# The first four blocks of a gated linear attention plus feed-forward kernel: loads split by tensor, stage list rewritten, y copied by ScalarE alone, two products of zeros at the start

## Chip, cores, metric

One core of one Trainium2 chip. The metric is the device time of one execution in microseconds; the kernel before takes 678.32 us (median of 678.15, 678.32 and 679.73).

## The reference

A linear attention with per-channel decay, written as a recurrence, then a feed-forward network with squared ReLU. All of it is float32; the weights come as float64 and are converted on the chip.

```python
# q, k, v, alpha: (B=4, H=8, S=768, D=48)
for t in range(S):
    state = alpha[:, :, t, :, None] * state + einsum('bhd,bhe->bhde', k[:, :, t], v[:, :, t])
    y[:, :, t] = einsum('bhd,bhde->bhe', q[:, :, t], state)
x = y.transpose(0, 2, 1, 3).reshape(3072, 384)
h = maximum(x @ w_in, 0)          # w_in (384, 2048)
out = (h * h) @ w_out             # w_out (2048, 384)
```

## The kernel before

The sequence is cut into 24 blocks of 128 steps (one chunk of one batch, all heads). A block has four stages: `decays` (transpose alpha, logarithm, running sum by a scan, two exponentials), `turn` (transpose q and k, scale them), `scores` (q times k, mask; k turned back into `ks`), `values` (state update `kv`, output `y`, copies of y into `xT`). Four blocks make a group of 512 tokens; while the feed-forward products of group g run, the stages of group g+1 are placed between them. Blocks 0 to 3 have no such products beside them: they are the start-up that this case is about. During the first feed-forward group (blocks 4 to 7) the weights are converted piece by piece, half on VectorE and half on ScalarE.

```python
NIN = 3; NV = 4; GB = 4; NR = 4
...
s_t = kept("s", B, [128, NP, 128])
for t in s_t:
    nc.vector.memset(t, 0.0)
...
def convert_first(i):          # a weight piece: DVE, DVE, then ACT, ACT
    nc.vector.tensor_scalar(out=power, in0=hi, ...)
    nc.vector.tensor_scalar(out=upper, in0=hi, ...)
    nc.scalar.activation(out=power, in_=power, func=AF.Relu, scale=2.0**23, bias=rebias)
    nc.scalar.activation(out=w, in_=lo, func=AF.Copy, scale=2.0**-52, bias=1.0)
def convert_second(i):         # then DVE three times
    nc.vector.scalar_tensor_tensor(out=power, ...)
    nc.vector.scalar_tensor_tensor(out=w, ...)
    nc.vector.tensor_tensor(out=w, in0=w, in1=power.bitcast(FP32), op=ALU.mult)

for n in range(NIN):
    load(n)                    # alpha, q, k, v of a block, 192 KB each
def next_weights():            # load piece, convert_second(i - 1), convert_first(i)
    ...
ident = consts.tile([128, 128], FP32, name="ident")
make_identity(nc, ident)       # POOL; every transpose needs it
...
def values(n):
    ...
    for p in range(NP):        # NP = 4 head pairs, one PSUM tile y
        copy = nc.scalar.copy if p < NP // 2 else nc.vector.tensor_copy
        for r, f, end in ((64, 2*p*D + 32, 2*(p + 1)*D), (0, 2*p*D, (2*p + 1)*D)):
            while f < end:     # 12 copies in all
                ...
                copy(out=xT[g][to:to+m, kk, t*C:(t+1)*C], in_=y[r:r+m, p, :])
...
order = [(0, 0), (0, 1), (1, 0), (0, 2), (1, 1)]
for n in range(2, GB):
    order += [(n - 2, 3), (n, 0), (n - 1, 2), (n, 1)]
order += [(GB - 2, 3), (GB - 1, 2), (GB - 1, 3)]
for n, s in order:
    stages[s](n)
    ...                        # further loads of inputs and weights
    if (n, s) in ((GB - 2, 3), (GB - 1, 2), (GB - 1, 3)):
        next_weights()
```

Of the kernel before, what the change touches and what calls it, by code (L numbers as in the profile page):

```python
# [8 lines left out]
FP32 = mybir.dt.float32  # L9
# [6 lines left out]
GB = 4  # L16
# [7 lines left out]
def kernel(  # L24
# [22 lines left out]
    nc = tc.nc  # L47
    B, H, S, D = q.shape
    C = 128
    NCH = S // C  # L50
    NP = H // 2
# [14 lines left out]
    ps_att = ctx.enter_context(tc.tile_pool(name="ps_att", bufs=4, space=PSUM))  # L66
# [4 lines left out]
    def kept(name, n, shape):  # L71
        return [consts.tile(shape, FP32, name=f"{name}{i}") for i in range(n)]

    NIN = 3
# [5 lines left out]
    tiles["v"] = kept("v_in", NV, [128, H * D])  # L80
    s_t = kept("s", B, [128, NP, 128])
    for t in s_t:
        nc.vector.memset(t, 0.0)


    srcs = {"a": alpha, "q": q, "k": k, "v": v}
# [1 line left out]
    def load(n, xs="aqkv"):  # L88
        c, b = divmod(n, B)
        for x in xs:  # L90
            t = tiles[x][n % len(tiles[x])]
            nc.sync.dma_start(
                out=t.rearrange("a (h d) -> a h d", h=H) if x == "v" else t[:, :, 0:D],
                in_=srcs[x][b, :, c * C : (c + 1) * C, :].rearrange("h s d -> s h d"),
            )
# [6 lines left out]
    def load_weights(i):  # L102
        dst = (w_in + w_out)[i]
        dt = moe_w_in.dtype
        raw = dst if dt == FP32 else raw_pool.tile(list(dst.shape), dt, tag="raw", name="raw")
        raws[i] = raw
        if i < NW:
            src = moe_w_in[:, i * DF // NW : (i + 1) * DF // NW]
            nc.sync.dma_start(out=raw, in_=src.rearrange("(k r) f -> r k f", r=128))
        else:  # L110
            i -= NW
            src = moe_w_out[i * DF // NW : (i + 1) * DF // NW, :]
            nc.sync.dma_start(out=raw, in_=src.rearrange("(j r) m -> r j m", r=128))
# [35 lines left out]
        )  # L149
        nc.vector.tensor_tensor(out=w, in0=w, in1=power.bitcast(FP32), op=ALU.mult)  # L150

    for n in range(NIN):
        load(n)
    to_load = list(range(2 * NW))
    stage = [0]

    def next_weights():
        i = stage[0]
        stage[0] += 1
        if NR - 2 <= i and to_load:  # L160
            load_weights(to_load.pop(0))
        if moe_w_in.dtype != FP32:
            if 0 < i <= 2 * NW:
                convert_second(i - 1)
            if i < 2 * NW:
                convert_first(i)


    nc.scalar.preload_act_table_set("natural_log_exp_and_others")
    ident = consts.tile([128, 128], FP32, name="ident")  # L170
    make_identity(nc, ident)
# [4 lines left out]
    nc.vector.memset(again[:, :, 0:1], 0.0)  # L176
    rebias = consts.tile([128, 1], FP32, name="rebias")
    nc.vector.memset(rebias, -896.0 * 2.0**23)
    NAM = 2
    am_t = kept("am", NAM, [128, 2, NP, 128])  # L180
    for t in am_t:
        nc.vector.memset(t, 0.0)


    bs, invs, qkT, ks, xT = {}, {}, {}, {}, {}
# [34 lines left out]
    def scores(n):  # L220
# [10 lines left out]
        for e in range(2):  # L231
            nc.vector.copy_predicated(  # L232
                out=am_t[n % NAM][:, e],
                mask=causal.bitcast(U32).unsqueeze(1).to_broadcast([128, NP, C]),
# [9 lines left out]
    def values(n):  # L244
        c, batch = divmod(n, B)
        qT = qkT.pop(n)[0]
        b = bs.pop(n)
        v_in = tiles["v"][n % NV]
        am = am_t[n % NAM]
        st = s_t[batch]  # L250
        kv = None
        if c < NCH - 1:
            kv = ps_att.tile([128, NP, 2 * D], FP32, tag="att", name="kv")
            kt = ks.pop(n)
            for p in range(NP):
                nc.tensor.matmul(  # L256
                    out=kv[:, p, :], lhsT=kt[:, p, :],
                    rhs=v_in[:, 2 * p * D : 2 * (p + 1) * D], start=True, stop=True,
                )
            pieces = []  # L260
            for e in range(2):
                rows = slice(64 * e, 64 * e + D)
                new = kv[rows, :, e * D : (e + 1) * D]
                old = st[rows, :, 80 * e : 80 * e + D]
                if c:
                    sm = p2.tile([128, NP, D], FP32, tag="sm", name="sm")
                    nc.vector.tensor_tensor(out=sm[rows], in0=new, in1=old, op=ALU.add)  # L267
                    new = sm[rows]
                pieces.append((old, new, b[rows, :, C - 1 : C].to_broadcast([D, NP, D])))

        y = ps_att.tile([128, NP, C], FP32, tag="att", name="y")
        if c:
            for p in range(NP):
                nc.tensor.matmul(  # L274
                    out=y[:, p, :], lhsT=st[:, p, :], rhs=qT[:, p, :],
                    start=(p == 0), stop=False, skip_group_check=True,
                )
        for p in range(NP):
            for e in range(2):
                nc.tensor.matmul(  # L280
                    out=y[64 * e : 64 * e + D + G * e, p, :],
                    lhsT=v_in[:, (2 * p + e) * D - G * e : (2 * p + e + 1) * D],
                    rhs=am[:, e, p, :], start=(c == 0 and p == 0), stop=True,
                    skip_group_check=True,
                )
        g, t = divmod(n, GB)
        if t == 0:
            xT[g] = x_pool.tile([128, KM, GB * C], FP32, tag="xT", name="xT")

        for p in range(NP):  # L290
            copy = nc.scalar.copy if p < NP // 2 else nc.vector.tensor_copy
            for r, f, end in ((64, 2 * p * D + 32, 2 * (p + 1) * D), (0, 2 * p * D, (2 * p + 1) * D)):
                while f < end:
                    kk, to = divmod(f, 128)
                    m = min(end - f, *(RUN[i % 128] for i in (r, to)))
                    copy(out=xT[g][to : to + m, kk, t * C : (t + 1) * C], in_=y[r : r + m, p, :])  # L296
                    r, f = r + m, f + m
        if kv is not None:
            for old, new, last in pieces:
                nc.vector.tensor_tensor(out=old, in0=new, in1=last, op=ALU.mult)  # L300
# [39 lines left out]


    stages = [decays, turn, scores, values]
    order = [(0, 0), (0, 1), (1, 0), (0, 2), (1, 1)]
    for n in range(2, GB):
        order += [(n - 2, 3), (n, 0), (n - 1, 2), (n, 1)]
    order += [(GB - 2, 3), (GB - 1, 2), (GB - 1, 3)]
    for n, s in order:
        stages[s](n)
        if (n, s) == (0, 1):
            load(3)  # L350
            load_weights(to_load.pop(0))
        if (n, s) == (1, 1):
            load(4, "a")
            load_weights(to_load.pop(0))
            load(4, "qk")
            load_weights(to_load.pop(0))
        if (n, s) == (0, 3):
            load(4, "v")
            load_weights(to_load.pop(0))
        if (n, s) in ((GB - 2, 3), (GB - 1, 2), (GB - 1, 3)):  # L360
            next_weights()

    NS = GB * len(stages)
    for g in range(NBLK // GB):
# [7 lines left out]
        for slot in range(NS):  # L372
            i, s = divmod(slot, len(stages))
            n = (g + 1) * GB + i
# [39 lines left out]
```

## Time and profile before

| | before |
|---|---|
| time, median of 3 | 678.32 us |
| profiled span, mean granted clock | 677.3 us, 0.977 |
| PE busy | 649.0 us (96%) |
| DVE, ACT busy | 275.2 us (41%), 194.4 us (29%) |
| first feed-forward product starts | 50.91 us |
| PE alone on the chain that ended last from | 118.50 us |

The shares of the whole span say little here, because they mix a start-up in which PE waits with a long stretch in which it never does. The view by slices shows the two: each digit is a fortieth of the span (17 us), in tenths. In the profile PE is TensorE, PEld its weight loads, DVE VectorE, ACT ScalarE, POOL GpSimd; PEclk is the clock granted to TensorE, as a share of full speed. Of the tiles, `la` is the logarithm of alpha and its running sum, `b` and `inv` the two exponentials, `am` the masked scores; `h` is the first feed-forward product, `r` its maximum with 0, `hid` the square of `r`, and `o` the second product.

```profile
PE   6768987999999999999999999999999999999998
PEclk9668999899999999999999999999999999999999
```

The first seven digits of PE are all there is to win; the other thirty-three are full, and the clock is full there too but for a dip in the eighth slice. The prediction shows the tables, waits and timelines that resolve those seven digits. In timeline lines the columns are start, length, engine, source line, operation, output and inputs, shape, count, and in brackets the idle time before and what ended it.

### The profile page before, as it was taken

To read this page: it belongs to the slowest core of one execution; us is meant where nothing else is said; L and a number is where in the kernel's file an instruction comes from. 1 tells how busy PE (TensorE), PEld (TensorE's weight loads), DVE (VectorE), ACT (ScalarE), POOL (GpSimd) and SP (SyncE) were. 2 spreads that over 40 slices of the span, in tenths; PEclk is the share of its full clock that TensorE was granted. 3 is DMA by queue.
4 is the path that set the end of the run, shared out by engine and by line. 5 is a ranking of instruction groups with operands and counts; after the bars stand their busy time and mean duration, and the time that the engine had idled before them with its cause. 6 is when DMAs were issued, how large, how long until landed. Compare 5 with 4: busy or idle time off the path is not lost.

```text
span 677.3 us, 7062 instructions
## 1 busy us (share of the span) xinstructions
PE 649.0 (96%) x2800; PEld 383.3 (57%) x2800; DVE 275.2 (41%) x505; ACT 194.4 (29%) x405; POOL 2.4 (0%) x17
## 2 busy tenths in 40 slices
PE   6768987999999999999999999999999999999998
PEld 5554544666555566554666655566645566644554
DVE  6658776865443331444422235412244422122100
ACT  3344666432332220332211223302223312122100
POOL 1000000000000000000000000000000000000000
PEclk9668999899999999999999999999999999999999
DMA  9916373800900012630003280003090000000000
GB/s 159 260 48 140 96 184 108 162 11 13 164 11 0 3 34 46 99 54 1 0 13 71 51 101 0 1 13 58 13 151 1 1 12 13 12 13 0 0 24 23
DMA packets 108705, 36.64 MB, mean 54 GB/s; under 512 B 100480, under 2 KB 103552, under 8 KB 108672
## 3 DMA queue, kind: packets, MB, share of 16 engines
q1 hardware_dynamic: 108672, 36.18, 28.4%
q8 instruction: 22, 0.36, 0.2%
q14 instruction: 11, 0.09, 0.0%
HBM read 31.46 MB, written 4.72 MB: 53 GB/s over the span
## 4 chain that ended last, share of the span: by engine, by line
PE 85%; DVE 8%; ACT 4%; issue 1%; DMA 1%; SPq 0%; DVEq 0%; ACTq 0%
PE o L326 37%; PE h L310 31%; PE y L280 3%; PE sc L226 3%; PE kv L256 2%; PE y L274 2%; PE kT L191 2%; DVE xT L296 2%; PE kr L240 2%; PE qT L191 1%; ACT xT L296 1%; DVE power L143 1%; PE aT L191 1%; DVE w_in L147 1%; DVE w_in L150 1%
## 5 line engine op out<-in xcount | busy, mean ns | idle before, releaser
L326 PE MATMUL o<-w_out,hid 128*128 128x384 f32 x768 | 257.7, 490 | 2.9 <-ACT r L315 2.9
L310 PE MATMUL h<-xT,w_in 128*128 128x512 f32 x576 | 256.9, 598 | 0.8 <-ACT xT L296 0.8
L326 PEld LDWEIGHTS o<-w_out,hid 128*128 128x128 f32 x768 | 143.4, 191 | 97.4 <-issue 3.7
L310 PEld LDWEIGHTS h<-xT,w_in 128*128 128x128 f32 x576 | 106.8, 191 | 122.6 <-issue 119.4
L319 DVE TENSOR_TENSOR hid<-r 128x512 f32<-128x512 f32 x80 | 55.4, 692 | 126.6 <-ACT r L315 126.3
L315 ACT ACTIVATE r<-h 128x512 f32<-128x512 f32 x96 | 56.9, 593 | 141.0 <-PE h L310 140.9
L296 DVE COPY xT<-y 32x128 f32<-32x128 f32 (+1 forms) x144 | 41.4, 288 | 83.5 <-ACT xT L296 80.6
L296 ACT COPY xT<-y 32x128 f32<-32x128 f32 (+1 forms) x144 | 37.1, 258 | 97.8 <-PE y L280 95.4
L334 ACT ACTIVATE osb<-o 128x384 f32<-128x384 f32 x24 | 11.8, 490 | 136.9 <-PE o L326 134.2
L232 DVE COPY_PREDICATED am<-causal,sc 128x512 f32<-128x512 uint32 x48 | 32.1, 723 | 42.9 <-PE sc L226 42.8
L201 DVE TENSOR_TENSOR_SCAN la<-again,la 128x512 f32<-128x512 f32 x24 | 29.3, 1222 | 32.5 <-ACT la L199 32.4
L226 PEld LDWEIGHTS sc<-qT,kT 48*128 48x128 f32 x384 | 24.7, 193 | 21.7 <-issue 11.8
L226 PE MATMUL sc<-qT,kT 48*128 48x128 f32 x384 | 29.8, 292 | 7.3 <-DVE kT L217 4.6
L256 PEld LDWEIGHTS kv<-v_in,ks 128*128 128x128 f32 x160 | 23.0, 212 | 11.7 <-ACT ks L242 6.7
L217 DVE TENSOR_TENSOR qT<-qT,b 128x512 f32<-128x512 f32 x24 | 16.6, 691 | 31.5 <-PE qT L191 30.4
L280 PE MATMUL y<-am,v_in 128*48 128x128 f32 (+1 forms) x384 | 28.5, 294 | 0.0
L135 ACT ACTIVATE power<-power,rebias 128x768 uint32<-128x768 uint32 x16 | 15.0, 936 | 46.5 <-DVE power L128 46.5
L256 PE MATMUL kv<-v_in,ks 128*128 128x96 f32 x160 | 23.7, 297 | 4.2 <-ACT ks L242 4.2
L267 DVE TENSOR_TENSOR sm<-kv,s 48x192 f32<-48x192 f32 x32 | 11.3, 354 | 38.7 <-PE kv L256 38.3
L208 ACT ACTIVATE b<-la 128x512 f32<-128x512 f32 x24 | 15.1, 630 | 35.9 <-DVE la L201 35.9
L280 PEld LDWEIGHTS y<-am,v_in 128*48 128x48 f32 (+1 forms) x384 | 22.4, 138 | 3.0 <-issue 0.5
L274 PE MATMUL y<-qT,s 128*128 128x128 f32 x160 | 21.6, 278 | 0.0
(42 smaller groups left out, 297.6 us busy)
## 6 DMA issues: line engine op xcount, KB each, us to landing
raw<-in_moe_w_in_dram SPq DMA_DIRECT2D x8, 768.0 KB, 5.4
raw<-in_moe_w_out_dram SPq DMA_DIRECT2D x8, 768.0 KB, 4.3
a_in<-in_alpha_dram SPq DMA_DIRECT2D x24, 192.0 KB, 4.9
q_in<-in_q_dram SPq DMA_DIRECT2D x24, 192.0 KB, 5.0
k_in<-in_k_dram SPq DMA_DIRECT2D x24, 192.0 KB, 4.9
v_in<-in_v_dram SPq DMA_DIRECT2D x24, 192.0 KB, 4.7
out_dram<-osb SPq DMA_DIRECT2D x24, 192.0 KB, 1.9
```

Source lines behind the costliest of these rows:

```text
L191: nc.tensor.transpose(out=ps[:, p, :], in_=rows[:, 128 * p : 128 * (p + 1)], identity=ident)
L201: nc.vector.tensor_tensor_scan(out=la.rearrange("a p t -> a (p t)"), data0=again.rearrange("a p t -> a (p t)"), data1=la.rearrange("a p t ...
L226: nc.tensor.matmul(out=ps[e][:, p, :], lhsT=kT[rows, p, :], rhs=qT[rows, p, :], start=True, stop=True,)
L232: nc.vector.copy_predicated(out=am_t[n % NAM][:, e], mask=causal.bitcast(U32).unsqueeze(1).to_broadcast([128, NP, C]), data=ps[e],)
L256: nc.tensor.matmul(out=kv[:, p, :], lhsT=kt[:, p, :], rhs=v_in[:, 2 * p * D : 2 * (p + 1) * D], start=True, stop=True,)
L274: nc.tensor.matmul(out=y[:, p, :], lhsT=st[:, p, :], rhs=qT[:, p, :], start=(p == 0), stop=False, skip_group_check=True,)
L280: nc.tensor.matmul(out=y[64 * e : 64 * e + D + G * e, p, :], lhsT=v_in[:, (2 * p + e) * D - G * e : (2 * p + e + 1) * D], rhs=am[:, e, p, ...
L296: copy(out=xT[g][to : to + m, kk, t * C : (t + 1) * C], in_=y[r : r + m, p, :])
L310: nc.tensor.matmul(out=ps, lhsT=w[:, kk, c0 : c0 + 128], rhs=xT[g][:, kk, :], start=(kk == 0), stop=(kk == KM - 1),)
L315: nc.scalar.activation(out=r, in_=ps, func=AF.Relu)
L319: nc.vector.tensor_tensor(out=hid[j], in0=r, in1=r, op=ALU.mult)
L326: nc.tensor.matmul(out=acc[t][:, 0:DM], lhsT=hid[j][:, t * C : (t + 1) * C], rhs=w_out[i][:, j % per, :], start=(j == 0), stop=(j == NJ - 1),)
```

## The change

The intent is to bring the first data to PE sooner, to keep PE's clock up while it waits for them, and to take VectorE's y copies out of the chain of the first groups. Its core (the moved loads of inputs and weights further down the start-up list are cut, and so is the move of `am`'s memsets to the front of VectorE's queue, which makes the zeros ready for the two products):

```diff
 for t in s_t:
-    nc.vector.memset(t, 0.0)
+    nc.gpsimd.memset(t, 0.0)
...
-for n in range(NIN):
-    load(n)
+for n, xs in ((0, "aqk"), (1, "a"), (0, "v"), (1, "qk"), (2, "a"), (1, "v"), (2, "qk")):
+    load(n, xs)
...
+for _ in range(2):
+    nc.tensor.matmul(
+        out=ps_att.tile([128, NP, C], FP32, tag="att", name="warm"),
+        lhsT=am_t[0][:, 0, 0, :], rhs=am_t[0][:, 0], start=True, stop=True,
+    )
...
-    for p in range(NP):
-        copy = nc.scalar.copy if p < NP // 2 else nc.vector.tensor_copy
+    for p in (1, 3, 0, 2):
+        on_scalar = p < NP // 2 or g < 2 and n != GB - 1
+        copy = nc.scalar.copy if on_scalar else nc.vector.tensor_copy
...
-order = [(0, 0), (0, 1), (1, 0), (0, 2), (1, 1)]
+order = [(0, 0), (0, 1), (1, 0), (0, 2), (1, 1), (0, 3)]
 for n in range(2, GB):
-    order += [(n - 2, 3), (n, 0), (n - 1, 2), (n, 1)]
+    order += [(n, 0), (n - 1, 2), (n, 1), (n - 1, 3)]
-order += [(GB - 2, 3), (GB - 1, 2), (GB - 1, 3)]
+order += [(GB - 1, 2), (GB - 1, 3)]
```

`g < 2` reaches further than the title's "first four blocks": blocks 4 to 7, the ones placed beside the first feed-forward group, get their y copies on ScalarE too. Only block 3 (`n == GB - 1`) and the blocks from 8 on keep the split, now in alternating order.

More of the change, by code (lines that the diff above doesn't have):

```diff
@@ L166, in next_weights @@
                 convert_first(i)
+    NAM = 2
+    am_t = kept("am", NAM, [128, 2, NP, 128])
+    for t in am_t:
+        nc.vector.memset(t, 0.0)
     nc.scalar.preload_act_table_set("natural_log_exp_and_others")
@@ L178 @@
     nc.vector.memset(rebias, -896.0 * 2.0**23)
-    NAM = 2
-    am_t = kept("am", NAM, [128, 2, NP, 128])
-    for t in am_t:
-        nc.vector.memset(t, 0.0)
+    for _ in range(2):
[3 more added lines that the diff above has]
+        )
     bs, invs, qkT, ks, xT = {}, {}, {}, {}, {}
@@ L349 @@
         if (n, s) == (0, 1):
-            load(3)
+            load(3, "a")
+            load(2, "v")
+            load(3, "qk")
+            load_weights(to_load.pop(0))
+            load(3, "v")
             load_weights(to_load.pop(0))
@@ L355 @@
             load(4, "qk")
+        if (n, s) == (0, 3):
             load_weights(to_load.pop(0))
-        if (n, s) == (0, 3):
             load(4, "v")
-            load_weights(to_load.pop(0))
         if (n, s) in ((GB - 2, 3), (GB - 1, 2), (GB - 1, 3)):
```

## The prediction

> **What bounds the kernel now.** I read the page first (PE busy 96% of the span), then a table of stretches, PE's waits, and the timeline engine by engine. The stretches are cut at the first FFN product (50.91 us) and where the chain that ended last becomes PE alone (118.50 us); columns are PE, PEld, DVE, ACT, POOL busy, granted clock, DMA share, GB/s.
>
> ```profile
> 0.00:50.91 50.91, 35.10 (x228) 28.25 (x228) 31.56 (x60) 19.83 (x45) 2.41 (x17) 0.76 0.84 155
> 50.91:118.50 67.59, 58.37 (x233) 30.54 (x233) 49.16 (x83) 39.57 (x69) 0.00 (x0) 0.98 0.52 132
> 118.50:677.30 558.80, 555.53 (x2340) 324.53 (x2340) 194.43 (x362) 135.04 (x293) 0.00 (x0) 1.00 0.21 35
> ```
>
> From 118.50 us PE idles 3.3 us in 559, at the very end, at full clock: nothing is to be had there. All gain must come as an earlier arrival at that point: PE idles 15.8 us before 50.91, often at half clock, and 9.2 us from there to 118.50. The waits between 51 and 119 us (total, times, longest):
>
> ```profile
> PE sc L226 <- DVE kT L217: 4.6, 2, 2.8
> PE o L326 <- ACT r L315: 2.9, 1, 2.9
> PE kv L256 <- ACT ks L242: 1.7, 2, 0.8
> PE h L310 <- ACT xT L296: 0.8, 1, 0.8
> ```
>
> PE waits for DVE and ACT, which wait for each other. One round of the first blocks, from the timeline (start, length, engine, line; at the end the idle time before it and its releaser):
>
> ```profile
> 27.02 1.64 ACT L296 COPY xT<-y 32x128 f32<-32x128 f32 x6 [4.01 <-PE y L280]
> 28.69 0.60 ACT L199 ACTIVATE la<-aT 128x512 f32<-128x512 f32 x1
> 28.70 1.85 DVE L296 COPY xT<-y 32x128 f32<-32x128 f32 x6 [4.62 <-ACT xT L296]
> 30.57 0.72 DVE L300 TENSOR_TENSOR s<-kv,b 48x192 f32<-48x192 f32 x2
> ...
> 31.33 1.23 DVE L201 TENSOR_TENSOR_SCAN la<-again,la 128x512 f32<-128x512 f32 x1
> ...
> 32.59 0.63 ACT L208 ACTIVATE b<-la 128x512 f32<-128x512 f32 x1 [3.30 <-DVE la L201]
> 33.12 0.61 ACT L210 ACTIVATE inv<-la 128x512 f32<-128x512 f32 x1
> ...
> 33.65 0.58 ACT L242 ACTIVATE ks<-kr 128x512 f32<-128x512 f32 x1
> ...
> 34.28 2.01 PE L256 MATMUL kv<-v_in,ks 128*128 128x96 f32 x8
> ```
>
> DVE's copies start when ACT's six have ended, and the scan, ready after la at 29.29, sits behind them and the s update until 31.33. Round: ACT copies, DVE copies, s, scan, b, inv, ks, kv, y. Starts of the copies: 15.80, 27.02, 37.83, so 11.2 and 10.8 us. In the first FFN group the same handover sits in a longer loop:
>
> ```profile
> 77.91 1.64 ACT L296 COPY xT<-y 32x128 f32<-32x128 f32 x6
> 85.49 0.94 ACT L135 ACTIVATE power<-power,rebias 128x768 uint32<-128x768 uint32 x1 [5.93 <-DVE power L128]
> 79.59 1.83 DVE L296 COPY xT<-y 32x128 f32<-32x128 f32 x6 [4.16 <-ACT xT L296]
> 90.16 1.22 DVE L201 TENSOR_TENSOR_SCAN la<-again,la 128x512 f32<-128x512 f32 x1 [4.25 <-ACT la L199]
> 96.41 1.16 PE L226 MATMUL sc<-qT,kT 48*128 48x128 f32 x16 [2.84 <-DVE kT L217]
> 118.50 4.54 PE L326 MATMUL o<-w_out,hid 128*128 128x384 f32 x8 [2.90 <-ACT r L315]
> ```
>
> DVE idles 4.16 us for ACT's copies, then ACT idles 5.93 us for DVE's conversion of a weight piece, then DVE 4.25 us for la, which stood behind both; PE pays last.
>
> **What the Trainium skill says.** "PSUM — Partial Sum Buffer", section "PSUM bank collisions raise a hardware error": two engines must not touch one bank and 32-partition quadrant at once, reads included. So the scheduler makes DVE wait for ACT on one y bank; the trace agrees, 0.03 us between ACT's end and DVE's start. Same page, "Engine vs sequencer instructions": ScalarE's and VectorE's queues are strict FIFO; the trace agrees (the scan held 2.0 us with its data there). "TensorE: Matmul & The Clock Gate", Part 1: the clock is at half until an activity window of 3.413 us was busy, the windows run free. Here four 128x128 transposes take 1.12 us or 0.66 us, and the switches near 13.2, 20.0, 26.9, 30.3, 37.1 and 40.5 us are multiples of 3.41 apart; in this run the page's rule holds. A window 79% busy (6.4 to 9.8, from the rows) did not warm. [...]DVE's memsets beside POOL's took their usual 0.9 ns per element.
>
> **The change, part by part.** I compared the built programs' order.
>
> Stages in another order: nothing. The two lists spell the same sequence of stages; PE's order differs only by the two added products. Only loads move.
>
> Loads: at the start each 192 KB tensor arrives about 1.1 us after the last. Block 1's alpha moves from fifth to fourth: about 7.3 instead of 8.4 us. But four memsets of s (512 elements) now stand on POOL before ident, which every transpose needs. POOL's 128-element memsets follow each other by 0.14 us and one-element ones by 0.03, so some 0.47 us each, 1.9 in all (estimate): ident at about 4.5 instead of 2.6, and the first transposes at 4.6 instead of 4.00. The next three groups then run without gaps. Scores of block 0: kT is ready at about 9.6 instead of 8.96, scores start 9.6 instead of 9.47. Near zero; with block 1's alpha early and a possible earlier warm clock I book -0.3.
>
> Products of zeros: 2 of 128x512 from about 1.9 us, 0.86 us each cold (1.7 us), before any data; they end near 3.6 and delay nothing. They fill half a window, then PE idles about 1 us for ident. Booked: 0.
>
> y on ACT alone, blocks 0 to 2: 12 copies x 0.27 = 3.28 us on ACT, then la 0.6, scan 1.23 (DVE has done s), b, inv and ks 1.7, kv 2.0, y 2.0: 10.9 us. Against 11.2 and 10.8, and since y2's product ran partly warm, I book -0.7 for both rounds. Scores and the next transposes no longer wait on DVE's copies, so PE's busy run before kv is longer and kv/y more often warm (0.9 less each): another -0.7.
>
> From the end of y2 to y3's copies: was 37.77 to 49.50 = 11.73, with DVE copies, s, and only then the weight conversion that ACT waits for. Now: copies 3.3, power/w_in 1.75 (DVE's half done meanwhile), ks 0.6, kv 2.0, y 2.0 = 9.7. -2.0.
>
> y3, and every block from 8 on: three copies each in turn, ACT, DVE, ACT, DVE. Each batch waits for the last instruction of the one before (same bank), so nothing overlaps and there are three handovers instead of one: +0.2 once; later PE has slack around them.
>
> Blocks 4 and 5, in the old times less the shift so far: ACT's copies end at 81.2; DVE, free at 75.4, does s and the conversion (2.75 us) and the next power at 79.6; ACT's power at 81.2 instead of 85.49; two r/hid pairs and la at 85.3 instead of 89.6; scan 85.9 instead of 90.16; kT at 92.1 instead of 96.4. PE is ready at 93.4: the wait of 2.84 is gone. By the same steps ks is ready at 99.95 and PE at 100.25 (0.85 gone), and the last two r of the group at 110.0 and 111.1 against PE's need at 111.5 (2.90 gone, and with it the half clock after it: 4.54 for 8 products where 2.7 is usual, 1.9). Sum 8.5; the margins are 0.3 to 1.3 us, so I book -8.0.
>
> Sum: -0.3 -0.7 -0.7 -2.0 +0.2 -8.0 = -11.5. 678.3 - 11.5 = **666.8 us**.
>
> **Rivals.** (1) ACT becomes the bound in the first FFN group: per block it gains 1.64 us and also carries r, the square and half the conversion. For: windows with ACT 8.92 and 9.38 of 10 us busy. Against: 5.6 to 6.4 of 10 on average, with idle stretches of 6 us. If so, r is late for the 4 PSUM buffers and only half of the 8 us comes: about 671. (2) The start decides: ident late by more than I estimate pushes everything, +1 us or more; or the zeros plus a gapless start warm PE one window earlier and the rounds drop to near 9.5 us, 2.5 us better: 664. (3) The alternating copies of blocks 8 on block ACT behind DVE so that r or hid come late in the saturated part. For: two more handovers in 16 blocks; against: no PE wait over 118 us today, DVE about 35% busy. 0.1 us each would cost 1.6: 668.5.
>
> **Range and chances.** Best terms together (start -1.1, rounds -2.6, then -2.2, -8.5) give 664; worst (start +0.5, rounds -0.4, -1.8, -5.5) 671. I take 662.5 to 671. The 2% line is 664.75, 2.1 us below my number, and needs the clock to come out well: 0.2. Slower by 2% has nothing that speaks for it: 0.01.
>
> **What would show it.** Right: the first FFN product near 48, DVE without L296 copies in blocks 0-2 and 4-7, no PE wait of over 0.5 us on kT, ks or r in blocks 5 to 7, stretch after that as long as before. The first transposes near 4.6 show the ident term. Wrong: a PE wait for r or ks that remains near 2 us (rival 1), first h at 50 or later (rival 2), PE idle in the stretch that is saturated now (rival 3).

## The result, and the profile after

Four runs of the changed kernel took 669.22, 667.80, 670.13 and 667.03 us: median 668.51, against 678.24 for the kernel before beside it. The ratio is 0.9856, interval 0.9824 to 0.9887: faster by 1.4%, inside the 2% that counts as the same. Ratios here are the mean time of one kernel's fast runs over that of the other's of the same rounds, so they are not quite the ratio of the medians quoted. 13 runs of this kernel have a mean of 667.97 us (standard deviation 1.08).

The slices of the changed kernel: the sixth and seventh digits of PE are nines now, and the dip of the clock in the eighth is gone; the first five hardly differ.

```profile
PE   7668999999999999999999999999999999999998
PEclk8769999999999999999999999999999999999999
```

The stretches, cut at the same two events as in the prediction: the first feed-forward product, and the ninth instruction of `o`, which waited for `r` until 118.50 in the kernel before (columns PE, PEld, DVE, ACT, POOL busy with instruction counts, granted clock, DMA share, GB/s):

```profile
0.00:50.69 50.69, 35.71 (x232) 28.37 (x233) 25.55 (x42) 24.51 (x63) 4.26 (x21) 0.76 0.83 156
50.69:110.43 59.74, 57.76 (x232) 30.79 (x233) 44.83 (x68) 44.38 (x83) 0.00 (x0) 0.97 0.66 156
110.43:667.40 556.97, 553.74 (x2341) 323.71 (x2339) 190.62 (x350) 135.93 (x301) 0.00 (x0) 1.00 0.20 35
```

The first stretch, at which most of the change is aimed, is 0.22 us shorter. The second is 59.74 us instead of 67.59: that is where most of the time came from. The third is 1.83 us shorter (556.97 against 558.80) with the same 3.2 us of PE idle: the eight instructions of `o` that took 4.54 us at half clock behind the wait for `r` are at full clock now (16 of them take 5.33). PE's waits between 49 and 119 us:

```profile
PE sc L233 <- DVE kT L224: 2.0, 1, 2.0
...
PE h L318 <- ACT xT L304: 1.7, 1, 1.7
```

The waits of the kernel before on r and ks (2.9 and 1.7 us) are gone, and of the 4.6 us for kT only block 4's 2.0 are left in this trace. The 1.7 us stand before the first feed-forward product. One round of the start-up now:

```profile
27.60 3.29 ACT L304 COPY xT<-y 64x128 f32<-64x128 f32 x12 [4.02 <-PE y L287]
30.91 0.60 ACT L206 ACTIVATE la<-aT 128x512 f32<-128x512 f32 x1
31.54 1.22 DVE L208 TENSOR_TENSOR_SCAN la<-again,la 128x512 f32<-128x512 f32 x1 [5.13 <-ACT la L206]
...
34.49 2.02 PE L263 MATMUL kv<-v_in,ks 128*128 128x96 f32 x8
```

ScalarE makes twelve copies in a row, VectorE does nothing for 5.13 us, and the scan starts 3.94 us after the first copy; before it started 4.31 us after it. So a round is only 0.37 us shorter up to the scan. The later group, the counterpart of the prediction's lines from 77.91 on:

```profile
76.34 3.29 ACT L304 COPY xT<-y 64x128 f32<-64x128 f32 x12
79.66 0.94 ACT L135 ACTIVATE power<-power,rebias 128x768 uint32<-128x768 uint32 x1
84.21 1.23 DVE L208 TENSOR_TENSOR_SCAN la<-again,la 128x512 f32<-128x512 f32 x1 [5.04 <-ACT la L206]
92.51 1.16 PE L233 MATMUL sc<-qT,kT 48*128 48x128 f32 x16
107.85 5.33 PE L334 MATMUL o<-w_out,hid 128*128 128x384 f32 x16
```

From the first copy to ScalarE's `power` it was 7.58 us (77.91 to 85.49) with 5.93 us of waiting; it is 3.32 us without a wait. The scan follows the first copy after 7.87 us instead of 12.25, the scores of block 5 no longer wait, and `o` starts 5.01 us earlier than before (107.85 instead of 112.86), its ninth instruction 8.07 us earlier (110.43 instead of 118.50).

The table splits the profiled difference of 9.9 us by the events that the prediction named (one trace each; how far its first row moves between traces of one kernel is shown under `after_again`):

| part | before | after | difference | predicted |
|---|---|---|---|---|
| start to y0's copies | 15.80 | 16.73 | +0.93 | -0.3 |
| two rounds, y0's to y2's copies | 22.03 | 21.72 | -0.31 | -1.4 |
| y2's to y3's copies | 11.67 | 9.55 | -2.12 | -2.0 |
| y3's copies | 3.55 | 3.60 | +0.05 | +0.2 |
| from there to the end | 624.25 | 615.80 | -8.45 | -8.0 |
| sum | 677.3 | 667.4 | -9.9 | -11.5 |

### The profile page after: what moved, and what is told of

The parts are those of the page before. It is cut to its first block, busy times and chain, and to the rows that moved or that the text cites. A ratio compares the mean times of both kernels' runs of the same rounds, so it can differ in the third digit from the quotient of the medians.

```text
span 667.4 us, 7057 instructions
## 1 busy us (share of the span) xinstructions
PE 647.2 (97%) x2804; PEld 382.9 (57%) x2804; DVE 261.0 (39%) x459; ACT 204.8 (31%) x447; POOL 4.3 (1%) x21
## 4 chain that ended last, share of the span: by engine, by line
PE 94%; ACT 3%; DVE 3%; issue 1%; ACTq 0%; DVEq 0%
PE o L334 37%; PE h L318 36%; PE y L287 4%; PE sc L233 4%; PE kv L263 3%; PE y L281 3%; PE kT L198 2%; ACT xT L304 2%; PE kr L247 2%; PE aT L198 1%; PE qT L198 1%; DVE la L208 1%; PE warm L186 1%; ACT la L206 0%; ACT power L135 0%
## 5 line engine op out<-in xcount | busy, mean ns | idle before, releaser
L304 ACT COPY xT<-y 64x128 f32<-64x128 f32 (+1 forms) x186 | 48.0, 258 | 116.7 <-PE y L287 96.8
L304 DVE COPY xT<-y 64x128 f32<-64x128 f32 (+2 forms) x102 | 29.4, 288 | 58.4 <-ACT xT L304 56.5
L233 PE MATMUL sc<-qT,kT 48*128 48x128 f32 x384 | 28.3, 287 | 4.0 <-DVE kT L224 4.0
```

What stands on the lines that cost most here:

```text
L233: nc.tensor.matmul(out=ps[e][:, p, :], lhsT=kT[rows, p, :], rhs=qT[rows, p, :], start=True, stop=True,)
L304: copy(out=xT[g][to : to + m, kk, t * C : (t + 1) * C], in_=y[r : r + m, p, :])
```

## The experiments

Theory: the handover on the y bank between ScalarE and VectorE is what the kernel lost, mostly in blocks 4 to 7, and taking VectorE's copies out gives nearly all of the gain; loads, zeros and copy order give nothing. Rivals: the gain comes from the start (loads, zeros); or the zeros work and something else takes their gain back. No run moves the loads alone: what they are worth is inside the result of a2. All runs were correct. Kernels of one call share a chip and the runs of the kernel before: a1, a2, a3 and a4 (before: median 678.76); `after_again` and the b kernels (679.42); `after_third`, `a3_again` and the c kernels (678.70).

### a1: of the change only the copies of blocks 4 to 7

```diff
 # kernel before
-copy = nc.scalar.copy if p < NP // 2 else nc.vector.tensor_copy
+on_scalar = p < NP // 2 or g == 1
+copy = nc.scalar.copy if on_scalar else nc.vector.tensor_copy
```

> The kernel before, with one part of the change alone: y of blocks 4 to 7 copied by ScalarE alone (12 copies in the old order); start, loads and blocks 0 to 3 stay as they were. My theory: this part gives the 8.4 us that the comparison of the traces puts down to blocks 4 and 5 (no PE wait on kT, ks or r in blocks 5 to 7, first o products without half clock), so about 678.2 - 8.4 = 669.8 us, with the first FFN product still at 50.9. Rival: the gain there needs the changed start as well (the memory loads in another order, or an earlier DVE), then under 4 us, 674 or more. Second rival: ScalarE becomes the bound, a PE wait on r of over 1 us appears.

Measured: 670.24 us (670.04, 667.78, 670.58, 670.44), ratio 0.9877 [0.985, 0.9904], which is 8.3 us. In its trace, of all waits of PE for VectorE or ScalarE after 60 us, one is left, that of block 4, and `o` starts at 108.67.

```profile
PE sc L226 <- DVE kT L217: 2.9, 1, 2.9
```

One condition on the kernel before does most of the work, though all of it lies after the blocks that the change was named for.

### a2: all of the change without that part

```diff
-on_scalar = p < NP // 2 or g < 2 and n != GB - 1
+on_scalar = p < NP // 2 or g < 1 and n != GB - 1
```

> The changed kernel with y of blocks 4 to 7 given back half to DVE (in turn 1,3,0,2 as elsewhere); everything else as changed. My theory: 8.4 us are lost again, about 677 us, and the PE waits on kT (2.8 us), ks and r (2.9 us) are back; what is left of the change in blocks 0 to 3 is worth about 1.5 us. Rival: blocks 0 to 3 carry more than 3 us, then 674 to 675 or less.

Measured: 675.85 us (675.63, 677.10, 675.54, 676.07), ratio 0.9971 [0.9946, 0.9996], which is 2.0 us. The waits between 60 and 125 us are back:

```profile
PE sc L233 <- DVE kT L224: 2.9, 2, 2.7
PE o L334 <- ACT r L323: 2.2, 1, 2.2
PE kv L263 <- ACT ks L249: 0.9, 1, 0.9
```

8.3 and 2.0 us add up to 10.3; the whole gives 9.8. It was run at another time. The two parts are nearly additive, and the rival that the start brings the gain has fallen: all that is done to blocks 0 to 3 is worth 2 us (0.3 to 3.7 by the interval).

### a3: the change without the products of zeros

```diff
-for _ in range(2):
-    nc.tensor.matmul(out=ps_att.tile(..., name="warm"), ...)
```

> The changed kernel without the two products of zeros. My theory: they cost time, for at half clock they take 3.78 us (two instructions per product, 0.86 us each), hold PE until 5.56 us and so delay the first transposes, which could start when ident is there, about 4.5 us. So the first transposes at 4.5 to 4.6 instead of 5.56, scores of block 0 at 9.6 instead of 10.55, all later about 1.0 us earlier: ratio to the changed kernel 0.9985, 667.5 us. Rival: the zeros earn their time by warming the clock (kT's four transposes 0.87, block 1's alpha 0.60 us instead of 1.1); without them those run at half clock and block 0's y copies begin no earlier than 16.7 us: same time or up to 1 us slower.

Measured: 666.36 us (666.38, 666.36, 665.94, 669.06, 665.62), ratio 0.9833 [0.9804, 0.9862]. In the changed kernel's trace the zeros are four PE instructions, not two, and they hold PE until 5.56 us:

```profile
1.99 3.78 PE L186 MATMUL warm<-am 128*128 128x512 f32 x4 [1.99 <-DVE am L172]
5.56 1.06 PE L198 MATMUL aT<-ident,a_in 128*128 128x128 f32 x4
```

Without them, the first transposes start when ident is there:

```profile
4.47 1.11 PE L191 MATMUL aT<-ident,a_in 128*128 128x128 f32 x4 [4.47 <-POOL ident masks.py:199]
...
9.51 1.16 PE L226 MATMUL sc<-qT,kT 48*128 48x128 f32 x16 [0.80 <-DVE kT L217]
```

So the zeros delay the first work on real data by 1.09 us, and in this trace the transposes alone had the clock up by 9.51: 16 score products take 1.16 us, which at half clock take 2.08. The median is 2.15 us below the first one of the changed kernel. It was run at another time.

### a4: no zeros, and ident ahead of the memsets on POOL

```diff
 # a3, and
-for t in s_t:                       # ahead of make_identity
-    nc.gpsimd.memset(t, 0.0)
 make_identity(nc, ident)
 ...
 make_upper_triangular(nc, causal, 1.0, diag=True)
+for t in s_t:
+    nc.gpsimd.memset(t, 0.0)
```

> As the run without zeros, and the four memsets of s moved on POOL behind ident and causal. My theory: ident is there at about 2.6 us as in the kernel before, the first transposes wait for alpha alone and start at 4.0 us, a further 0.5 us earlier than without zeros alone: about 667.0 us, and in block 0 about 1.5 us less than the changed kernel. Rival: the kT product of block 0 is bound elsewhere (its load, or ScalarE's inv), and less than 0.2 us comes of it.

Measured: 667.28 us (667.03, 668.26, 667.28, 667.27), ratio 0.9844 [0.982, 0.9868]: no faster than a3. The first transposes start at 4.07 and the scores 0.43 us earlier than in a3's trace, at 9.08, but at half clock (2.08 us), and y0's copies start at 15.30 instead of 14.54. What ident gains is less than what the clock decides; it can't be read from these times.

### after_again: the changed kernel once more

No edit.

> The changed kernel itself once more, beside the runs below, so that they are compared on one chip. 668.5 us within 1.5; a ratio to the kernel before near 0.9856. It also tells how far the times of one and the same kernel differ with the moment at which the clock's activity window falls: two traces of it should show the zeros warming PE at different transposes.

Measured: 667.29 us (666.83, 667.75, 666.55, 667.92), ratio 0.9823 [0.9809, 0.9836], profiled span 665.0. The trace explains a spread of over 2 us between runs of one kernel. The same zeros, ending at the same time, are followed by transposes at full clock here:

```profile
5.56 0.60 PE L198 MATMUL aT<-ident,a_in 128*128 128x128 f32 x4
```

In the first trace they took 1.06. There the scores of block 0 came at 10.55 in 1.49 us, here at 10.09 in 1.16, and kv at 12.89 instead of 14.59; y0's copies start at 15.10 instead of 16.73, and the 1.6 us stay until the first feed-forward group (y3's copies at 46.18 instead of 48.00). The rounds themselves are nearly the same, 10.86 and 10.67 us here, 10.87 and 10.85 there: kv takes 2.01 to 2.02 us in all four. So most of what these two runs differ by in the start-up came before y0's copies. I call this the phase: the clock switches at steps of 3.41 us, as in the prediction's trace, and where the steps fall differs from run to run (the first drop to half clock comes at 11.2 us in the first trace and at 19.2 here).

The phase also decides how block 4's late kT shows. Its scores wait 0.26 us here instead of 1.98, but the twelve `h` instructions that open the group took 7.22 us, partly at half clock, instead of 5.52. From the first `h` to these scores it is 13.50 us here and 13.53 there: kT sets it in both.

### b2: four products of zeros instead of two

```diff
-for _ in range(2):
+for _ in range(4):
```

> The changed kernel with four products of zeros instead of two: the suspected cost doubled. My theory: their PE time is not free, for ident is there at 4.5 us; four of them end between 7.3 us (half of them at full clock) and 8.9 us (all at half clock), and the first transposes wait as long: they start 1.8 to 3.4 us later than with two (5.56). Part comes back because the clock is then certainly full, so that block 0 takes up to 1.5 us less: 1 to 3 us slower than the changed kernel. Rival: the warm clock is worth more than it costs: no slower, or faster.

Measured: 669.14 us (668.85 to 669.62), ratio 0.9851 [0.9838, 0.9865], against 0.9823 [0.9809, 0.9836] for two: 1.9 us slower. In its trace the first transposes start at 8.20 instead of 5.56 and y0's copies at 18.95, later than in any trace with two. Part came back, as expected: in the second round kv and y ran at full clock, and the round took 9.08 us (29.81 to 38.89) instead of 10.67 to 10.85.

```profile
36.70 1.13 PE L263 MATMUL kv<-v_in,ks 128*128 128x96 f32 x8 [0.24 <-ACT ks L249]
37.76 1.09 PE L287 MATMUL y<-am,v_in 128*48 128x128 f32 x16
```

By the times, more zeros cost more than they bring.

### b3: block 3's y on ScalarE too

```diff
-on_scalar = p < NP // 2 or g < 2 and n != GB - 1
+on_scalar = p < NP // 2 or g < 2
```

> The changed kernel with the exception for block 3 taken away: its y too goes through ScalarE alone. My theory: the copies end after 3.3 instead of 3.6 us, and DVE, which now does s and the second conversion at 48.7 instead of 52.4 us, lets la, scan and the kT product of block 4 come about 4 us earlier, so PE's wait there (1.98 us) and the half clock after it (7.01 us for the h that take 5.32) go: 3 to 4 us less than the changed kernel, about 665. Rival: the exception was made because ScalarE is the late one there; then the power for the next weight comes later, la no earlier, and nothing or less than 1 us is gained.

Measured: 665.20 us (668.16, 664.44, 666.36, 663.62, 665.20), ratio 0.9788 [0.9772, 0.9804], against 0.9823 for the changed kernel: 2.4 us faster, less than the 3 to 4 expected. The wait of PE that the change had left, block 4's scores for kT, goes. With y3's copies off VectorE, its second half of the weight conversion runs at 48.71 instead of 52.37, and the scan of block 4 behind it comes earlier:

```profile
55.13 1.23 DVE L208 TENSOR_TENSOR_SCAN la<-again,la 128x512 f32<-128x512 f32 x1 [2.66 <-ACT la L206]
...
64.83 1.16 PE L233 MATMUL sc<-qT,kT 48*128 48x128 f32 x16
```

The same two of the changed kernel (first trace):

```profile
57.96 1.23 DVE L208 TENSOR_TENSOR_SCAN la<-again,la 128x512 f32<-128x512 f32 x1 [1.83 <-ACT la L206]
...
64.22 1.16 PE L233 MATMUL sc<-qT,kT 48*128 48x128 f32 x16 [1.98 <-DVE kT L224]
```

b3's trace was even taken with y0's copies at 18.29, 1.56 us later than in the other, and still its `o` starts at 106.76 against 107.85. From the first `h` to block 4's scores it is 12.76 us instead of 13.53.

### b4: the copies in the old order of p

```diff
-for p in (1, 3, 0, 2):
+for p in range(NP):
```

> The changed kernel with the pieces of y in the old order 0,1,2,3 (block 3 and all blocks from 8 on: ScalarE's six and then DVE's six, instead of threes in turn). My theory: nothing overlaps in either order because both read one PSUM bank; block 3 takes 3.55 instead of 3.60 us, its first FFN product starts about 1 us earlier (near 49.7) but must then wait for DVE all the same; in the later blocks PE has slack: within 0.5 us of the changed kernel. Rival: the handovers of the alternating order cost in 16 blocks 0.1 us each, then 1.5 us faster; or the alternating order was made for a gain, then slower by over 1 us.

Measured: 669.36 us (669.40, 669.32, 668.05, 669.45), ratio 0.9849 [0.9836, 0.9863]; the changed kernel 0.9823 [0.9809, 0.9836]. The traces don't explain 1.8 us by the order: b4's trace and the first of the changed kernel run in step to 0.01 us (y0's, y1's and y2's copies at 16.73, 27.59, 38.44 against 16.73, 27.60, 38.45), and their spans are 667.6 and 667.4. Its first feed-forward product starts 1.1 us earlier (49.55), and PE then waits 2.94 us instead of 1.98 for the scores of block 4. At equal phase the order is worth 0.2 us; whether the rest of the timed difference is the phase of those four runs stays open.

### after_third and a3_again: with and without zeros

No edit, and a3's edit.

> The changed kernel a third time, as the measure beside the three runs below on one chip: 667.9 us, the mean of its eight runs so far, within 1.5.

> The changed kernel without the zeros, now beside the changed kernel. So far five runs without them have a mean of 666.7 us and eight with them 667.9, from different calls. My theory, with the spread that the moment of the clock window gives: about 1 us less than the changed kernel of this call; in the trace the first transposes at 4.5 instead of 5.56. Rival: the zeros make a favourable window more likely, and with them in the same call the two are equal within 0.3 us, or the changed kernel is faster.

Measured: with zeros 667.99 us (666.74 to 669.19), ratio 0.985 [0.9831, 0.9869]; without 667.33 us (666.25 to 668.00), ratio 0.9833 [0.9813, 0.9853]. The intervals overlap. a3_again's trace shows why one look at a3 was not enough: here the transposes did not warm the clock in time.

```profile
9.51 2.08 PE L226 MATMUL sc<-qT,kT 48*128 48x128 f32 x16 [0.89 <-DVE kT L217]
```

y0's copies start at 16.19 in it and at 14.54 in a3: the same 1.6 us of phase as with zeros. Phase for phase the kernel without zeros is 0.5 us ahead (14.54 against 15.10; 16.19 against 16.73). Pooled, 9 runs without have a mean of 666.92 us and 13 with them 667.97; 1.05 us is about two standard errors (0.48, from deviations of 1.12 and 1.08). The zeros gain nothing in any comparison; whether they cost 0.5 or 1 us is not settled.

### c6 and c7: what the experiments point to

c6 is a3 and b3 together. c7 adds another spacing of the weight conversions in the start-up:

```diff
-if (n, s) in ((GB - 2, 3), (GB - 1, 2), (GB - 1, 3)):
-    next_weights()
+# once at (GB - 1, 2), twice at (GB - 1, 3)
```

> A version meant to beat both: no zeros, and y of block 3 too through ScalarE alone. Each took something off by itself (zeros about 1.2 us over different calls; block 3 2.4 us beside the changed kernel). If they add: 3 to 4 us less than the changed kernel, about 664.3 us, 2.1% under the kernel before. Rival: they act on the same wait of PE for block 4's kT, which a start that comes 1 us earlier already shortens; then no more than the 2.4 us of block 3 alone.

> As the run above, and the first weight conversion is put behind block 3's scores, the second behind its y, so that ScalarE makes ks of block 3 right after y of block 2 and not after 1.75 us of conversion. PE's wait for that ks, 3.9 us in the trace of the changed kernel, should fall to about 2.1 and the first FFN product come 1.7 us earlier. What comes of it in the end is open: the conversions shift behind, la of block 4 waits for two of them, so that PE's wait for block 4's kT may come back with 1 us or more. 0 to 1.7 us less than the run above; if that wait comes back in full, nothing or slower.

Measured: c6 664.14 us (663.96, 662.89, 665.26, 664.14, 665.24), ratio 0.9791 [0.9769, 0.9813]. It is 4.0 us faster than the changed kernel in the same call and 2.9 than a3_again. PE, busy 67.33 of the 70 us from 50 on in the first trace of the changed kernel, has no gap left there, at full clock:

```profile
50.00:120.00 70.00, 70.00 (x298) 39.28 (x298) 54.33 (x78) 49.94 (x92) 0.00 (x0) 1.00 0.67 161
```

c7: median of the four fast runs 663.13 us (666.23, 662.49, 662.52, 663.74), ratio 0.9781 [0.9754, 0.9809]; its profiled run was slow (964.36 us at a clock of 0.653) and is not used. It can't be told from c6. Both beat the kernel before and the changed one: the change's exception for block 3 cost it time, and its zeros gained it nothing.

## Why the prediction was right, and where it was not

**The class and the range held**: 666.8 us predicted, 668.51 measured first, 667.97 over 13 runs.

**Blocks 4 and 5 (-8.0): right in size and cause.** a1 gives 8.3 us alone, a2 loses it, and the waits named (kT of block 5, ks, r) are the ones that went and came back. The trace of the change shows 8.45 for this part, next to the 8.5 that was worked out before the margin was taken off. The clock moved too, but cancels: the first twelve feed-forward instructions took 7.06 us before and 5.52 in this trace, the twelve behind block 4's scores 5.32 before and 7.01 now.

**y2 to y3 (-2.0): the interval shrank as predicted**, by 2.12 us between the two traces. No run isolates it, so its cause is argued from the trace; a2's 2.0 us are the sum of all but the copies of blocks 4 to 7.

**y3's copies (+0.2): too small to matter as a span (+0.05), but the wrong question.** The cost of leaving y3 split was not its handovers. It was VectorE, tied to ScalarE for that time, which could not do the weight conversion ahead of block 4's scan; b3 shows this to be worth 2.4 us. The prediction worked such a step out for block 5 and did not look at block 4, where the kernel before had the other 1.8 us of its two waits for kT.

**The rounds: the "10.9 us" worked out was right (10.87 and 10.85), the -0.7 booked for it was not, and the -0.7 of clock did not come.** Two rounds of 10.9 against 11.2 and 10.8 give -0.2, and -0.31 was measured. The step "PE's busy run before kv is longer and kv/y more often warm" failed: kv takes 2.01 to 2.02 us in both rounds in all three traces of the changed kernel. That it can happen, b2's round of 9.08 us shows; no trace with two zeros has it. y2's product, which ran partly warm before (1.55 us), took 1.98 in the first trace and 1.79 in the others, so a little was even lost there. PE is still idle for 3.1 and 2.3 us of the two rounds (7.78 us busy of 10.87, 8.52 of 10.85), where the kernel before had 2.5 in the first (8.75 of 11.22). One reading behind this was off too: the window from 6.4 to 9.8 us that did not warm was 69% busy (2.36 of 3.40 us), not 79%.

**The start (-0.3): +0.93 in the first trace, -0.70 and -0.73 in the two others, so the phase outweighs the term.** The ident term was right: POOL's four memsets took 1.92 us where 1.9 was estimated, and a3's first transposes start at 4.47 where 4.6 was said. What failed is the step on the zeros, "0.86 us each cold ... they end near 3.6 and delay nothing". 0.86 us is about what a product of this shape takes at full clock: twelve instructions of the feed-forward, which are six such products, take 5.32 us in the first trace, 0.89 each. A 128x512 product of float32 is two PE instructions, and at half clock it takes twice that. The four measured took 3.78 us and the next product starts at 5.56, past ident. The rival that the zeros could warm PE a window earlier was right as to mechanism in two of three traces (transposes of 0.60 us from 5.56), but the rounds stayed at 10.66 to 10.87 us, and with PE idle for 1.74 to 1.98 us for kT just after, y0's copies start later than without zeros in either phase.

**"First FFN product near 48": 50.69 in the first trace, 48.86 and 48.82 in the others, though the sum didn't use it.** In the first trace the start and the rounds brought y3's copies only to 48.00. From there it took 2.69 us where it had been 1.41: the products need the first piece of `xT`, and in the new order of p its two parts are copied by ScalarE before and after VectorE's turn.

**The rivals**: ScalarE did not become the bound (no wait of PE for r is left, and none appears in c6, where block 3's other six copies are on it as well); the alternating copies from block 8 on cost nothing (PE idle in the last stretch 3.2 us as before); the start did not decide: all but the copies of blocks 4 to 7 is worth 2.0 us in a2, and the phase moves y0's copies by 1.6 us.

## What to carry to other kernels

When two engines share the copies out of one PSUM tile and the scheduler makes them take turns, giving all of them to one engine costs that engine some time but unties the other; look for what stands behind the copies in the other engine's queue, since the gain (8 us here, where 1.6 us of copying a block moved) is in that queue and not in the copies. No run gave all copies to VectorE instead, so the choice of ScalarE is not shown to be the better one. Ask this for every block that meets saturated work, and not just for the ones in the start-up that look idle. Compare versions that differ by under 2 us only at equal phase of the clock or over many runs, because one kernel's traces differed by 2.4 us with no edit at all.

## What the Trainium skill lacked or had wrong

- "TensorE: Matmul & The Clock Gate", Part 2, "Back-to-back issue gap" has spacings for 128 and 512 columns but none for float32 (another page counts the passes of a float32 product, without a time). Here a 128x512 float32 product is two PE instructions and takes 0.89 us at full clock (six in 5.32); four instructions took 3.78 us at the start, mostly at half clock. Whether this lack led to the mis-sized zeros is not shown.
- The same page, Part 4, says that the full clock does not engage for transpose mode. Here float32 transposes ran in 0.60 us for four at full clock and 1.11 at half, and in one trace (a3) transposes alone, from 4.47 to 8.7 us, were followed by score products at full clock (1.16 us for 16). In another trace of that kernel (a3_again) they were not (2.08 us). Counting back in steps of 3.41 us from the first drop of the granted clock gives the windows: in a3 the one from 5.41 to 8.83 was 95% busy (3.25 of 3.42 us), in a3_again those from 3.77 to 7.18 and on to 10.59 were 79% and 73% busy (2.71 and 2.48 us).
- No page has a rate of POOL's memset: four of 128x512 float32 took 1.92 us, 0.48 each, in front of the identity that every transpose waited for.
